# Sums of squares of four token tiles on ScalarE instead of TensorE, in a fused linear-attention and bilinear block

## The chip, the cores and the metric

The kernel runs on one core of a Trainium2 chip. The metric is device time in microseconds, of the whole kernel. A core has five engines with instruction queues of their own: TensorE (PE in the profile, with PEld for its weight loads), VectorE (DVE), ScalarE (ACT), GpSimd (POOL) and SyncE (SP), which here only issues transfers. Each works its queue off in order; they wait for each other through semaphores.

## The reference, cut to what matters

One batch of 2048 tokens of width 640 goes through a linear attention with 32 heads of 20 channels and a bilinear feed-forward of width 1536, both with a layer norm ahead and a residual around. All arrays are bf16.

```python
def _layernorm(x, axis=-1, eps=1e-5):
    m = jnp.mean(x, axis=axis, keepdims=True)
    v = jnp.var(x, axis=axis, keepdims=True)
    return (x - m) / jnp.sqrt(v + eps)
...
    qkv = (x @ wqkv) -> q, k, v per head
    pq = jnp.einsum("bhsd,hdf->bhsf", q, w_phi)
    pk = jnp.einsum("bhsd,hdf->bhsf", k, w_phi)
    phi_q = jnp.concatenate([_softmax(pq), _softmax(-pq)], axis=-1)
    phi_k = jnp.concatenate([_softmax(pk), _softmax(-pk)], axis=-1)
    kv = jnp.einsum("bhsf,bhsd->bhfd", phi_k, v)
    num = jnp.einsum("bhqf,bhfd->bhqd", phi_q, kv)
    o = num / den;  A(x) = o @ wo
    B(x) = ((x @ w_gate) * (x @ w_up)) @ w_down
...
    h = x + A(_layernorm(x));  h2 = h + B(_layernorm(h))
```

## The kernel before, in words

**Tiles.** Tokens are cut into 16 tiles of 128. A tile stands in the core's memory twice: `x_all` holds it as it is (tokens along the partitions), `xT` transposed (channels along the partitions), which is what a matmul needs. Both come from the same input by transfers that SP issues: `load_x(b)` brings four tiles of `x_all` at a time (units lx0 to lx3), `load_xT(t)` one transposed tile (units lT4 to lT15; tiles 0 to 3 are in unit "in").

**Statistics** (`stats`, units s0, s2, s4, s8, s12; the number is the first tile). The layer norm of the input needs a mean and a sum of squares per token. For most tiles TensorE multiplies a tile's transposed block by itself with a column of ones appended (128x129): the last column gives the sum, the diagonal the squares, and VectorE adds the diagonal up (L702). For the tiles in `ST_ACT` TensorE makes the sum alone (128x1), and ScalarE squares and sums the row from `x_all` (`act_sum`, L650). GpSimd then computes the scale from both (L707 to L719).

**Weights.** The key weights are folded with w_phi first (`wk_rounds`). Unit wk takes the mean of the key weights' rows and transposes them on TensorE (L746); two of the five blocks are copied out by VectorE (L784) and ScalarE (L787), the rest with the mean taken off (L803, L806). Meanwhile w_phi arrives as `Wrows`, by a transfer that stands in ScalarE's queue, and is spread into five block-diagonal pieces `Phi` by VectorE (three) and GpSimd (two), L636 in unit "in". Units x0 to x4 multiply the transposed key weights by `Phi`; x0 and x1 do so in two steps, the second with the mean repeated by GpSimd (L777). `evac` (L861, L864) writes the folded weights to `Wp`. The query weights follow the same way later (wm, wq, y0 to y4), value weights are centred by c0 to c4.

**Keys, values, queries.** Unit k (`keys`) multiplies a tile by the folded key weights, VectorE takes the row maximum (L925) and ScalarE two exponentials (L933); unit K normalises on VectorE and GpSimd. Unit v is the values, q and Q the queries, whose features go through two transposes on SP's queue (L1003). Units A sum keys times values over all tokens, then n, h, f and D are the attention's output, its projection, the feed-forward up and down.

**Order.** What runs when isn't found by the hardware: `ORDER` lists, for each engine, the units in sequence; where a unit has several instructions on an engine, its name stands several times and they are taken in the order in which the program makes them. In ScalarE's list "in" therefore means, in turn, the transfer of key weights, the transfer of `Wrows`, and one Exp on a column of ones (L612) that gets the table of functions loaded:

```python
load_wnat(1, (3, 5), "ACT", at=4.3)
load(Wrows[:, :, :], A_w_phi.rearrange(...), [R_Wrows], 0.03, eng="ACT", at=5.35)
...
g.op("ACT", lambda e: e.activation(out=junk[:, 0, 0:1], in_=ones[:, 0:1], func=ACT.Exp), ...)
```

`place` walks through the lists with assumed durations (`t`, `lat`, and for transfers `size`), to give buffers away; four double banks of matmul results (`p_ps`) are the scarcest. A transfer with `at` is taken there to arrive at that time, wherever its issue stands: `land = o.at or max(s + 2.3, fabric) + o.bytes`. `finish` then puts in the semaphores.

Of the kernel before, what the change touches and what calls it, by code (L numbers as in the profile page):

```python
# [11 lines left out]
P = 128  # L12
S = 2048
D = 640
NT = S // P
NC = D // P
# [41 lines left out]
ST_ACT = (12,)  # L58
# [39 lines left out]
    "DVE":  # L98
# [16 lines left out]
    "ACT":  # L115
# [318 lines left out]
def _build(ctx, nc, A_x, A_wqkv, A_w_phi, A_wo, B_w_gate, B_w_up, B_w_down, out):  # L434
    g = Prog(nc, ctx)
# [8 lines left out]
    x_all = sb([P, NT, D], BF16, "x_all")  # L444
# [1055 lines left out]
```

## Time and profile before

| what | value |
|---|---|
| median of 3 runs | 267.84 us (267.67 to 268.1) |
| the profiled execution | 267.55 us, span 265.8 us |
| TensorE busy | 260.4 us, 98% of the span |
| VectorE / ScalarE / GpSimd busy | 222.7 / 177.2 / 190.1 us |
| share of TensorE in the chain that ended last | 85% |
| granted clock of TensorE | 0.999 |
| transfers | 28.65 MB, mean 108 GB/s |

The span runs from the first to the last instruction of the profiled execution; its own time includes what lies around it. A busy share is an average over stages. The stages by time: weights up to about 12 us, keys, values and first queries up to 74 us, attention output and queries mixed with the feed-forward of the first 512 tokens up to about 150 us, then the feed-forward.

In timeline rows the columns are: start and length in us, engine, line, operation, result <- inputs, shape, count, and in brackets the idle time ahead of it with what ended it. A row can merge several instructions, and matmuls overlap, so that the step from start to start is what they cost. In the table by windows they are: window, its length, busy time and instruction count of PE, PEld, DVE, ACT and POOL, granted clock, share and rate of the transfers.

### The profile page before, as it was taken

The page shows a single profiled execution, that of the slowest core. Times are in us where ns is not written, and L with a number is a line of the kernel's source. Part 1 is how long each engine was busy: PE and PEld are TensorE (multiplying, and loading weights), DVE is VectorE, ACT ScalarE, POOL GpSimd, SP SyncE. Part 2 cuts the span into 40 slices and gives each one's busy share as a digit, 9 for nine tenths or more (in the row PEclk, how much of TensorE's full clock was granted, in tenths as well). Part 3 has the DMA queues.
Part 4 walks back from the last instruction along what each step waited for, and adds up shares of the span by engine and source line. Part 5 has one row for each costly group of instructions (what it writes and reads, how often), then busy time and mean ns, then how long its engine had stood idle before and what let it go on. Part 6 is the DMA issues. An engine that isn't in the chain of part 4 may idle for free.

```text
span 265.8 us, 6243 instructions
## 1 busy us (share of the span) xinstructions
PE 260.4 (98%) x2418; PEld 200.0 (75%) x2433; DVE 222.7 (84%) x417; ACT 177.2 (67%) x387; POOL 190.1 (72%) x243
## 2 busy tenths in 40 slices
PE   8999999999999999999999999999999999999995
PEld 8877777776877787777767887777777777777773
DVE  1999999999999876998999778988778788675683
ACT  2567999999857998769553695764857555645220
POOL 5446989999932889999974789359866575648652
PEclk9999999999999999999999999999999999999999
DMA  7997999903155789666856515300410401001012
GB/s 188 302 138 175 165 233 401 382 32 75 39 82 100 89 247 210 130 106 133 131 115 128 47 25 79 99 4 0 56 45 19 83 0 52 1 2 51 14 65 71
DMA packets 67390, 28.65 MB, mean 108 GB/s; under 512 B 57632, under 2 KB 66080, under 8 KB 67360
## 3 DMA queue, kind: packets, MB, share of 16 engines
q1 hardware_dynamic: 66432, 27.90, 48.7%
q10 hardware_dynamic: 928, 0.35, 0.5%
q8 instruction: 19, 0.31, 0.5%
q14 instruction: 11, 0.09, 0.1%
HBM read 11.82 MB, written 2.62 MB: 54 GB/s over the span
## 4 chain that ended last, share of the span: by engine, by line
PE 85%; DVE 5%; DMA 3%; ACT 3%; issue 1%; POOL 1%; SPq 0%; ACTq 0%
PE ps L657 60%; PE ps L1210 24%; DMA phiqT<-eq 3%; ACT eq L933 1%; DVE ob L1075 1%; PE ps L746 1%; DVE x_all L1093 1%; DVE ps L925 1%; DVE Sq L987 1%; ACT phiqT L1335 0%; POOL eq L999 0%; DVE rden L1073 0%; DVE phiqT L806 0%; ACT junk L650 0%; ACT eq L1220 0%
## 5 line engine op out<-in xcount | busy, mean ns | idle before, releaser
L657 PE MATMUL ps<-Wp,xT 128*128 128x320 bf16 (+1 forms) x606 | 89.1, 299 | 0.0
L657 PEld LDWEIGHTS ps<-Wp,xT 128*128 128x128 bf16 x606 | 58.0, 98 | 22.5 <-ACT phik L933 0.3
L1240 POOL TENSOR_TENSOR phik<-phik,gate 128x512 bf16<-128x512 bf16 x34 | 40.1, 1184 | 25.9 <-DVE phik L1237 25.5
L1220 ACT ACTIVATE eq<-ps 128x256 f32<-128x256 f32 x110 | 37.4, 386 | 23.0 <-PE ps L1210 18.6
L1210 PE MATMUL ps<-phik,Wgu 128*128 128x256 bf16 (+1 forms) x214 | 46.6, 299 | 0.2
L950 POOL TENSOR_TENSOR phik<-phik,Rk 128x1280 bf16<-128x1280 bf16 x16 | 37.4, 2357 | 5.8 <-DVE Rk L949 4.8
L657 PE MATMUL ps<-phik,Wgu 128*128 128x256 bf16 (+1 forms) x259 | 33.2, 280 | 0.1
L657 PEld LDWEIGHTS ps<-phik,Wgu 128*128 128x128 bf16 x260 | 25.0, 98 | 5.5
L1337 POOL TENSOR_TENSOR phiqT<-phiqT,x_all 128x320 f32<-128x320 f32 x26 | 21.7, 844 | 9.7 <-ACT phiqT L1335 9.6
L925 DVE TENSOR_REDUCE ps<-ps 128x1 f32<-128x640 f32 (+1 forms) x32 | 26.1, 818 | 2.8 <-PE ps L657 2.8
L1210 PEld LDWEIGHTS ps<-phik,Wgu 128*128 128x128 bf16 x228 | 21.9, 98 | 5.7 <-ACT eq L1220 0.2
L657 PE MATMUL ps<-vaug,phik 128*128 128x63 bf16 (+1 forms) x308 | 25.9, 238 | 0.0
L987 DVE TENSOR_REDUCE Sq<-eq 128x66 f32<-128x1320 bf16 x16 | 24.2, 1513 | 1.4 <-ACT eq L933 1.4
L1237 DVE TENSOR_TENSOR phik<-ps,eq 128x512 bf16<-128x512 f32 x28 | 19.1, 687 | 6.3 <-PE ps L1210 6.2
L1335 ACT ACTIVATE phiqT<-ps 128x320 f32<-128x320 f32 x26 | 11.4, 437 | 19.3 <-PE ps L657 19.2
L947 DVE TENSOR_REDUCE Ssum<-phik 128x64 f32<-128x1280 bf16 x16 | 23.3, 1460 | 0.0
L1235 DVE TENSOR_TENSOR gate<-ps,eq 128x512 bf16<-128x512 f32 x27 | 18.5, 685 | 5.2 <-PE ps L1210 2.9
L657 PEld LDWEIGHTS ps<-vaug,phik 128*128 128x128 bf16 x308 | 18.1, 97 | 5.3
L999 POOL TENSOR_TENSOR eq<-eq,rq 128x660 bf16<-128x660 bf16 x16 | 20.9, 1305 | 0.8
L933 ACT ACTIVATE eq<-ps,nb,rs 128x300 bf16<-128x300 f32 (+2 forms) x26 | 17.2, 689 | 6.1 <-DVE nb L928 4.5
L1342 DVE TENSOR_TENSOR outb<-ps,phiqT 128x320 bf16<-128x320 f32 x28 | 13.4, 487 | 6.9 <-PE ps L657 5.5
L1139 ACT ACTIVATE gate<-ps 128x256 bf16<-128x256 f32 (+1 forms) x26 | 10.4, 406 | 10.3 <-PE ps L657 9.6
(168 smaller groups left out, 526.2 us busy)
## 6 DMA issues: line engine op xcount, KB each, us to landing
x_all<-in_A_x_dram SPq DMA_DIRECT2D x4, 640.0 KB, 10.7
out_dram<-outb SPq DMA_DIRECT2D x14, 160.0 KB, 1.9
Wgu<-in_B_w_gate_dram SPq DMA_DIRECT2D x1, 1920.0 KB, 10.6
Wgu<-in_B_w_up_dram SPq DMA_DIRECT2D x1, 1920.0 KB, 16.3
vaug<-in_B_w_down_dram SPq DMA_DIRECT2D x1, 1920.0 KB, 8.5
Wp<-in_A_wqkv_dram SPq DMA_DIRECT2D x1, 800.0 KB, 5.0
phiqT<-in_A_wqkv_dram SPq DMA_DIRECT2D x1, 800.0 KB, 6.4
Wo<-in_A_wo_dram SPq DMA_DIRECT2D x1, 800.0 KB, 6.0
```

The lines of the kernel that those rows point to most:

```text
L657: ins = e.matmul(o_, lhsT=l_, rhs=r_, start=s_, stop=p_, skip_group_check=True)
L925: g.op("DVE", lambda e: e.tensor_reduce(out=mx(), in_=src(), axis=AX.XY if len(src().shape) == 3 else AX.X, op=ALU.max, apply_absolute_val ...
L933: g.op("ACT", lambda e, s=s, sc=sc, to=to, of=of: e.activation(out=to(s), in_=of(), func=ACT.Exp, bias=nb[:, i:i + 1], scale=sc[:, t:t + 1 ...
L947: g.op("DVE", lambda e: e.tensor_reduce(out=Ssum[:, vs.i, :], in_=x, axis=AX.X, op=ALU.add), rd=R_phik[t], wr=vs.R, use=[vs], t=1.39, lat=1.5)
L950: g.op("POOL", lambda e: e.tensor_tensor(out=x, in0=x, in1=Rk[:, vr.i, :].unsqueeze(2).to_broadcast([P, 2 * H, DH]), op=ALU.mult), rd=vr.R ...
L987: g.op("DVE", lambda e: e.tensor_reduce(out=Sq[:, vs.i, :].rearrange("p (w g) -> p w g", w=NQ), in_=feat(0, NQ).rearrange("p w (g f) -> p ...
L999: return e.tensor_tensor(out=x, in0=x, in1=rq[:, vr.i, :].rearrange("p (w h) -> p w h", h=HW).unsqueeze(3).to_broadcast([P, NQ, HW, DH]), ...
L1210: ins = e.matmul(o_, lhsT=l_[0](c), rhs=m_, start=fr, stop=False, skip_group_check=True)
L1220: g.op("ACT", lambda e: e.activation(out=half(s[i], 256 * h, 256 * (h + 1)), in_=PS[v.i][:, bk, 256:512], func=ACT.Copy), rd=[v.R[bk]], wr ...
L1237: g.op("DVE", lambda e: e.tensor_tensor(out=hhT[:, hb_, ft, :], in0=PS[v.i][:, 1, :], in1=half(s[1]), op=ALU.add), rd=[v.R[1]] + s[1].R, w ...
L1240: g.op(eng, lambda e: e.tensor_tensor(out=hhT[:, hb_, ft, :], in0=hhT[:, hb_, ft, :], in1=gate[:, vg.i, :], op=ALU.mult), rd=R_out + vg.R, ...
L1337: g.op("POOL", lambda e: e.tensor_tensor(out=slot(x), in0=slot(x), in1=x_all[:, t, c], op=ALU.add), rd=x.R + [R_h[t]], wr=x.R, use=[x], t= ...
```

## The change

`ST_ACT` gains tile group 8: tiles 8 to 11 get their sums of squares from ScalarE on `x_all` instead of from 128x129 products on TensorE and diagonal sums on VectorE. All five queues get a new order. Some of the assumed durations of `place` change (transfers are taken to land earlier, transposes to occupy less), which can change which buffer a unit gets, and nothing else that runs. Of the order the beginnings are shown, and SP's in full up to the queries; the later stages exchange neighbours.

```diff
-ST_ACT = (12,)
+ST_ACT = (8, 12)
...
     "PE":
-        "warm wk wk wk wk wk wk wk wk wk s0 wk x1 s0 x1 x3 wv wv x2 x0 x0 s2 x4 s2 k0 k0 k0 k0 k0 k3 k1 wm k2 v2 v3 s4 s4 s4 s4 "
-        "v5 k7 v7 k4 k6 v4 k5 y3 v0 y1 s8 s8 s8 s8 y4 k10 y2 y0 v1 s12 s12 k11 q0 s12 s12 k8 k9 v11 q1 v9 v6 k12 k13 v14 v10 v13 "
+        "warm wk wk wk wk wk wk wk wk wk wk s0 x1 s0 x1 x0 x3 x0 wv wv x2 x4 s2 s2 k0 k0 k0 k0 k0 k3 k1 wm v2 k2 v3 s4 s4 s4 s4 "
+        "k7 v5 v7 k4 v4 y3 k6 v0 y1 k5 s8 s8 s8 s8 y0 v1 y2 k10 y4 k11 s12 s12 s12 q0 s12 v11 k8 k9 v9 q1 k12 k13 v10 v14 v6 k14 "
...
     "DVE":
-        "wk in in wk in wk wk wk s0 s0 x1 x3 s0 c2 c1 c0 s2 s2 c4 s2 k0 k0 c3 k3 k3 k1 k1 K0 k2 wq2 wq4 K0 K1 k2 s4 s4 s4 s4 s4 "
+        "wk in in in wk wk wk wk s0 s0 s0 x3 x1 c1 c0 c2 s2 s2 k0 s2 k0 c3 c4 k3 k3 k1 wq2 k1 K0 k2 K0 k2 K1 s4 s4 s4 s4 s4 K3 k7 "
...
     "ACT":
-        "in in in wk wk wk x2 x0 x4 k0 k0 k3 wm k1 k1 v2 v3 k3 k2 wq1 k2 v5 wq3 k7 v7 k7 k4 k4 v4 k6 k6 k5 v0 k5 s12 y4 y2 s12 y0 "
+        "in wk in wk wk x0 x2 x4 in k0 k0 wm k3 k3 k1 v2 k1 wq1 v3 k2 s8 k2 s8 wq3 v5 k7 v7 k7 v4 k4 k4 s8 v0 s8 k6 k6 y0 k5 v1 "
...
     "POOL":
-        "in in in in in in in in in in in in pad in in wk s0 s0 s0 in in s0 s2 s0 s2 s2 s0 s2 s2 s2 K0 s4 s4 s4 s4 s4 s4 K3 K1 K2 "
+        "in in in in in in in in in in in in in in in wk s0 s0 s0 in s0 s0 in s2 s0 s0 s2 s2 s2 s2 s2 pad K0 s4 s4 s4 s4 s4 s4 K3 "
...
     "SP":
-        "in in in in in in in lwq t4 lT7 lT4 t2 lT5 lT6 t3 t1 t0 lx3 lT10 lT15 lT9 lT11 lT8 lT13 lT14 lT12 lx0 lwo lg lu lx2 lx1 "
-        "Q0 Q1 Q0 Q1 Q2 Q2 Q3 Q3 Q5 Q5 n2 n3 Q7 Q7 Q4 ld Q4 Q6 n7 n5 Q6 Q8 Q8 h3 n4 h2 Q10 Q10 n6 Q14 Q14 Q9 n8 Q9 h5 h7 Q11 Q11 "
+        "in in in in in in in t2 lwq lT6 t4 lT5 t1 lT4 lT7 lx2 t3 t0 lT14 lT10 lx0 lT11 lT9 lT8 lx3 lT13 lT12 lwo lT15 Q0 lg Q0 "
+        "lx1 Q1 lu Q1 Q2 Q2 Q3 Q3 Q5 n2 Q5 n3 Q7 Q7 ld Q4 Q4 Q6 n7 n5 Q6 h3 h2 Q8 Q8 n4 Q10 Q10 n6 Q14 Q14 n8 Q9 Q9 h7 h5 Q11 Q11 "
...
-        return g.op(eng, lambda e: e.dma_start(out_, in_), wr=wr, dma=("w", 8), t=0.5, lat=0.4 if at else 1.9, size=mb / 0.38, at=at)
+        return g.op(eng, lambda e: e.dma_start(out_, in_), wr=wr, dma=("w", 8), t=0.5, lat=0.4 if at else 0.6, size=mb / 0.38, at=at)
-    def transpose(out_, in_, rd, wr, use=(), t=1.27, size=1.07, lat=0.5, at=0.0):
+    def transpose(out_, in_, rd, wr, use=(), t=1.27, size=0.45, lat=0.3, at=0.0):
...
```

In the SP list "t" are transposed loads of query weights, lwq and lwo the query and output weights, lg, lu and ld the gate, up and down weights. The code of `stats` is the same; tiles 8 to 11 take its other branch.

More of the change, by code (lines that the diff above doesn't have):

```diff
@@ L587, in load_xT @@
     def load_xT(t, at=0.0):
-        transpose(lambda: xT[:, t, :, 0:P], lambda: A_x[0, P * t:P * (t + 1), :], [], [R_xT[t]], t=1.5, size=0.75, lat=1.25 if at else 2.75, at=at)
+        transpose(lambda: xT[:, t, :, 0:P], lambda: A_x[0, P * t:P * (t + 1), :], [], [R_xT[t]], t=1.5 if at else 1.4, size=0.75 if at else 0.62, lat=1.25 if at else 2.1, at=at)
     def load_x(b):
-        load(x_all[:, 4 * b:4 * b + 4, :], A_x[0, 4 * P * b:4 * P * (b + 1), :].rearrange("(t p) n -> p t n", p=P), [R_x[b]], 1.2)
+        load(x_all[:, 4 * b:4 * b + 4, :], A_x[0, 4 * P * b:4 * P * (b + 1), :].rearrange("(t p) n -> p t n", p=P), [R_x[b]], 0.9)
     def load_wv(c0, c1, at):
@@ L686, in f @@
                 return mms(e, lst)
-            g.op("PE", f, rd=[R_xT[t], R_one, R_xone], wr=[v.R[j // 2]], use=[v], t=0.125 if act else 0.282, lat=0.275 if act else 0.43)
+            g.op("PE", f, rd=[R_xT[t], R_one, R_xone], wr=[v.R[j // 2]], use=[v], t=0.19 if act else 0.282, lat=0.34 if act else 0.43)
             if act:
@@ L818, in wq_means @@
         v = Buf(p_ps, 2)
-        g.op("PE", lambda e: mms(e, mean_mms(PS[v.i][:, 0, :], range(NC), 0)), rd=R_Wnat + [R_one], wr=v.R, use=[v], t=0.64, lat=0.79)
+        g.op("PE", lambda e: mms(e, mean_mms(PS[v.i][:, 0, :], range(NC), 0)), rd=R_Wnat + [R_one], wr=v.R, use=[v], t=0.73, lat=0.88)
         g.op("ACT", lambda e: e.activation(out=nmeanq[:, :], in_=PS[v.i][:, 0, 0:NC], func=ACT.Copy, scale=-1.0 / SC),
@@ L1003, in queries @@
             SLOT_USERS.append(transpose(lambda w0=w0, w1=w1: phiqT[:, bb, w0:w1, P * tt:P * (tt + 1)], lambda w0=w0, w1=w1: eq[:, b.i, P * w0:P * w1],
-                      b.R + [R_pad], [R_phiqT[bb][k][tt]], [b], t=0.254 * (w1 - w0), size=0.214 * (w1 - w0)))
+                      b.R + [R_pad], [R_phiqT[bb][k][tt]], [b], t=1.3, size=0.5, lat=0.35))
     KVBUF = Buf(p_ps, 2)
@@ L1371, in wqT @@
         U("t%d" % a)
-        transpose(lambda: WT[:, 0, a, :], lambda: A_wqkv[:, P * a:P * (a + 1)], [], [R_WT[0][a]], t=1.5, size=0.75, lat=2.75)
+        transpose(lambda: WT[:, 0, a, :], lambda: A_wqkv[:, P * a:P * (a + 1)], [], [R_WT[0][a]], t=1.4, size=0.62, lat=2.1)
     U("warm")
@@ L1385, in _build @@
     U("lwo")
-    load(Wo[:, :, 0:D], A_wo.rearrange("(c p) n -> p c n", p=P), R_Wo, 1.5)
+    load(Wo[:, :, 0:D], A_wo.rearrange("(c p) n -> p c n", p=P), R_Wo, 0.95)
     for b in range(NB):
```

121 rows, old and new, of the table ORDER are left out of this document.

## The prediction

> **What bounds the kernel now.** I read the page first (busy shares, then the chain that ended last), then the table by windows for the stretch of keys and values, and then the timelines of single engines over the first 17 us, where the new order changes most.
>
> ```profile
> span 265.8 us, 6243 instructions
> PE 260.4 (98%) x2418; PEld 200.0 (75%) x2433; DVE 222.7 (84%) x417; ACT 177.2 (67%) x387; POOL 190.1 (72%) x243
> PE 85%; DVE 5%; DMA 3%; ACT 3%; issue 1%; POOL 1%; SPq 0%; ACTq 0%
> ...
> 20.00:40.00 20.00, 19.94 (x196) 15.30 (x194) 19.57 (x48) 18.16 (x27) 16.20 (x18) 1.00 0.87 193
> 40.00:60.00 20.00, 20.00 (x157) 14.28 (x155) 20.00 (x32) 18.99 (x30) 19.46 (x19) 1.00 0.72 268
> 60.00:74.00 14.00, 14.00 (x240) 11.25 (x238) 13.38 (x23) 12.01 (x20) 13.84 (x9) 1.00 0.27 54
> ```
>
> The reader should see two things. TensorE (PE) is the bound from end to end: 85% of the chain is its own work. And between 20 and 74 us VectorE (the third busy figure in a row, behind PE and PEld; ScalarE and GpSimd follow) is full too: 19.57 + 20.00 + 13.38 = 52.95 of 54 us. A microsecond in which TensorE stands still at the start therefore has no later slack to vanish in: it moves the end by a microsecond.
>
> **Part 1: twenty matmuls become narrow.** For tiles 8 to 11 the 128x129 products give way to 128x1 sums, as tiles 12 to 15 (s12) have them already.
>
> ```profile
> 34.13 1.30 PE L657 MATMUL ps<-xT 128*128 128x129 bf16 x20
> 35.26 0.48 PE L657 MATMUL ps<-Phi,phiqT 128*128 128x140 bf16 x6
> ...
> 39.20 0.39 PE L657 MATMUL ps<-ones,xT 128*128 128x1 bf16 x10
> 39.61 2.93 PE L657 MATMUL ps<-Wp,xT 128*128 128x320 bf16 x20
> 42.38 0.39 PE L657 MATMUL ps<-ones,xT 128*128 128x1 bf16 x10
> 42.63 1.11 PE L657 MATMUL ps<-Wp,xT 128*128 128x320 bf16 x7
> ```
>
> Start to start, s8 takes 35.26 - 34.13 = 1.13 us now. The same twenty in s12 take 0.41 + 0.25 = 0.66 us (at the faster of the two rates, 0.50). TensorE gains 0.47 to 0.63 us; I take **-0.5**. VectorE loses four diagonal sums. Each is 0.28 us long (the first row below), so four give back up to 1.1 us. That pays nothing while TensorE is full, but it keeps VectorE from becoming the bound.
>
> ```profile
> 13.28 0.28 DVE L702 CUSTOM_DVE_ANT_0 t<-ps,ident 128x128 f32<-128x128 f32 x1
> ...
> 36.23 0.74 ACT L650 ACTIVATE junk<-x_all 128x640 bf16<-128x640 bf16 x1
> 36.95 1.30 ACT L861 ACTIVATE Wp<-ps 128x640 bf16<-128x640 f32 x2
> ```
>
> **Part 2: ScalarE gets four squares.** One costs its queue 36.95 - 36.23 = 0.72 us, four 2.9 us, placed among keys 2, 7, 4 and 6. The table above leaves ScalarE idle for 20 - 18.16 = 1.84 us from 20 to 40, for 2.85 us from 20 to 60. So the cover just about holds: the cost lies between 0 and 2.9 - 1.84 = 1.1 us (if keys wait for their exponentials and TensorE for the banks behind them). I take **+0.1**, what is left over the idle of 20 to 60.
>
> The squares read x_all of tiles 8 to 11. That load stood behind lu and moves up in SP's queue, past twelve of the transposes that load xT and past lx3, lx0, lwo, lg and lu: seven transposes and lwq are left ahead of it behind the first seven entries.
>
> ```profile
> 22.46 0.58 SPq L549 DMA_DIRECT2D x_all<-in_A_x_dram  x1
> DMA to landing us min/median/max: 4.7/10.7/17.1
> ```
>
> The first x_all load went out at 22.46 us behind nine transposes and lwq; with two of about 1.3 us fewer this one goes out near 20. The four such loads took 4.7 to 17.1 us; the long ones went out behind the gate and up weights, which no longer stand ahead, so I take 4.7 and a landing near 25. The first square stands behind the first exponential of key 2, near 23.5 us plus the delay of part 3, so 27: zero. Without that delay ScalarE would wait up to 1.5 us.
>
> **Part 3: the load of Wrows now stands behind a waiting activation.** This decides. ScalarE's old order begins "in in in wk wk wk", the new one "in wk in wk wk x0 x2 x4 in". Of ScalarE, "in" is three things in this order: a load of key weights (L549), the load of Wrows (L549), the Exp that brings the table (L612). The first "wk" is the copy at L787. So the issue of Wrows moves behind L787, and ScalarE works in order.
>
> ```profile
> 0.78 0.46 ACTq L549 DMA_DIRECT2D phiqT<-in_A_wqkv_dram  x1
> 1.28 0.49 ACTq L549 DMA_DIRECT2D Wrows<-in_A_w_phi_dram  x1
> 1.80 1.28 ACT L612 ACT_TABLE_LOAD   x1 [1.80 <-issue]
> 6.44 0.70 ACT L787 ACTIVATE phiqT<-ps 128x640 bf16<-128x640 bf16 x1 [3.15 <-PE ps L746]
> 15.50 0.88 ACT L933 ACTIVATE phik<-ps,nb,rs 128x640 bf16<-128x640 f32 x1 [2.19 <-DVE nb L928]
> ...
> phiqT<-in_A_wqkv_dram ACTq DMA_DIRECT2D x1, 320.0 KB, 3.9
> Wrows<-in_A_w_phi_dram ACTq DMA_DIRECT2D x1, 25.0 KB, 4.6
> ...
> DMA to landing us min/median/max: 2.6/4.4/6.6
> ```
>
> L787 waits for TensorE's transposes until 6.44 us. So Wrows, now issued at 1.28 us and landed at 1.28 + 4.6 = 5.9 us, goes out between 6.44 us (behind the start of L787) and 7.14 us (behind its end). I take 6.5. How long it flies: 4.6 us was behind the 320 KB of its own queue, which landed at 0.78 + 3.9 = 4.7 us; the shortest of the early transfers takes 2.6 us (last line, the transposes). I take the middle, 3.6 us, and get a landing at **10.1 us**, bounds 6.44 + 2.6 = 9.0 and 7.14 + 4.6 = 11.7.
>
> The Trainium skill, "DMA: Bandwidth & Descriptors", section "Queues, rings and completion order", says that each DMA engine takes turns between the queue rows it has work for, packet by packet. By that rule the backlog of SP's queue would hardly hold the small load on ScalarE's row up, and the landing would lie at the lower bound of 9.0 us, with a delay of 2.4 us in place of the 3.5 us below.
>
> What waits for Wrows:
>
> ```profile
> 5.98 0.86 POOL L636 TENSOR_TENSOR Phi<-Wrows,G 128x140 bf16<-128x140 bf16 x2 [1.93 <-DMA Wrows<-in_A_w_phi_dram]
> 6.15 0.85 DVE L636 TENSOR_TENSOR Phi<-Wrows,G 128x140 bf16<-128x140 bf16 x2
> 7.36 0.17 DVE L775 TENSOR_SCALAR nmean<-ps 128x5 f32<-128x5 f32 x1 [0.36 <-PE ps L657]
> 7.44 0.32 DVE L636 TENSOR_TENSOR Phi<-Wrows,G 128x160 bf16<-128x160 bf16 x1
> 7.59 0.74 POOL L777 CAST outb<-nmean 128x640 bf16<-128x640 f32 x1 [0.75 <-DVE nmean L775]
> 7.86 0.47 PE L657 MATMUL ps<-Phi,phiqT 128*128 128x140 bf16 x6
> 8.17 0.45 PE L657 MATMUL ps<-xT 128*128 128x129 bf16 x5
> 8.45 0.48 PE L657 MATMUL ps<-Phi,outb 128*128 128x140 bf16 x6
> 9.14 0.47 PE L657 MATMUL ps<-Phi,phiqT 128*128 128x140 bf16 x6 [0.21 <-DVE sm L698]
> ```
>
> The first folded matmul of x1 (7.86 us) needs all five Phi pieces, three of them on VectorE. In the new order VectorE does the three in a row ahead of nmean: 0.85 + 0.32 us, plus some 0.1 for the two hand-overs, 1.25 us after the landing. x1 starts at 10.1 + 1.25 = 11.35 us, **3.5 us later** than 7.86 (bounds: 9.0 + 1.25 and 11.7 + 1.25, that is +2.4 and +5.1). TensorE has nothing else to do meanwhile: its queue holds s0 once ahead of x1, as before at 7.18 us, and s0, x1, x0, x3 and the value-weight sums behind it. nmean, now queued on VectorE behind the late Phi pieces, makes the cast at L777 late in turn: nmean and cast take 0.17 + 0.74 us after Phi, while TensorE has the first x1 and s0, 0.31 + 0.28 us, so a stall of about 0.3 us comes. It replaces the one ahead of 9.14 us (0.21 idle, and the pitch of 0.69 from 8.45), and I cost the difference at nothing. What follows, x0 to x4, s2 and key 0, moves as a block.
>
> The Exp with its table moves behind x4. The first activation is then L787, and the load of 1.28 us can stand ahead of it in ScalarE's 3.15 us of idle time. If it came behind L787's wait, Wrows would be later by 1.28 us; if it came ahead of key 0 it would lie in the 2.19 us before 15.50. Zero, inside the bounds.
>
> **Part 4: loads of gate and up weights.** lg, lx1 and lu now go out between the transposes of Q0 and Q1, and ld ahead of Q4's.
>
> ```profile
> 59.28 7.78 SPq L553 DMA_TRANSPOSE phiqT<-eq  x4
> 94.10 8.54 DMA phiqT<-eq
> 74.87 0.53 PE L657 MATMUL ps<-Phi,phiqT 128*128 128x42 bf16 x12 [0.29 <-DVE Phi L1040]
> L657 PE MATMUL ps<-phik,Wgu x150: 270/272/275, 85.6 to 120.9; 128*128 128x256 bf16 x150
> ```
>
> A transpose behind a big load lands late, 8.54 us (here behind ld). Q1's second half, issued by 59.28 + 7.78 = 67.1 us at the latest, would then land by 75.6; its user at 74.87 us moves to about 78. The gate weights, first used at 85.6, have 18 us. Zero; without the 3 us of delay up to 0.8 us.
>
> **Part 5: the rest of the order.** In all five queues many neighbours change places, the later stages included; the work is the same. TensorE is idle for 265.8 - 260.4 = 5.4 us of the whole span, the wait of 0.82 us at its start among it, so a better order can win little and a worse one has no row here to price it. I take zero, with 0.6 us either way in the range.
>
> **The sum.** The profiled execution took 267.55 us (span 265.8 and 1.75 around it), 0.29 under the median of 267.84. 267.55 + 3.5 - 0.5 + 0.1 = 270.65, so a median of **270.9 us**, 1.2% slower. With the bounds: 267.84 + 2.4 - 0.63 = 269.6, and 267.84 + 5.1 - 0.47 + 1.1 = 273.6.
>
> **Rivals.** *Not slower: the load is issued ahead of the wait.* If L787's wait holds only the arithmetic and the queue goes on to the next issue, Wrows still leaves near 1.3 us and the change is worth part 1: 267.84 - 0.5 = 267.3. For it: no separate semaphore instruction stands ahead of L787. Against: ScalarE's first three rows follow one another in order and none overlaps its predecessor's issue. It decides as soon as Wrows lands by about 6.5 us. Chance 0.10.
>
> *The clock falls.* TensorE would be idle from about 7.9 to 11.35 us. Early on it ran slowly:
>
> ```profile
> 0.82 4.21 PE L657 MATMUL ps<-const-bfloat16-1.0 128*128 128x128 bf16 x38 [0.82 <-PEq L1485]
> ```
>
> 38 matmuls of 128 columns in 4.21 us are 111 ns each; later the twenty of 129 columns in s8 take 1.13 us, 56 ns each. If the idle time sent TensorE back to that rate for as long as at the start (some 4 to 5 us), half of it would be lost: 2.0 to 2.5 us more, 273.1 us. Against: a stretch of that idle length is nowhere in this trace, so nothing shows it. Chance 0.10. The Trainium skill, "TensorE: Matmul & The Clock Gate", part 1, says that an idle window of about 3.4 us halves the clock and that the window runs freely; the idle time above is about that long, so it would be caught whole in few cases, and I keep the chance small.
>
> *ScalarE becomes the bound.* The squares find no gaps, and the whole 1.1 us of part 2 is paid: 267.84 + 3.5 - 0.5 + 1.1 = 271.9. For it: 18.99 of 20 us busy from 40 to 60. Against: 1.84 + 1.01 + 1.99 = 4.8 us idle from 20 to 74. Chance 0.10.
>
> **How the numbers follow.** Forecast 0.70, rivals 0.10 each. A measurement of this kernel tells changes of about 0.2% from none. Slower by more than that: forecast, clock and ScalarE, 0.90. The first rival ends at -0.2%, split into 0.06 faster and 0.04 same. Range 269.0 to 273.2: from the lower bound of the load's flight, less the 0.6 us of part 5, to the clock case; the upper bound of 273.6 needs every cost at its worst.
>
> **What would show it.** Wrows issued at 6.5 us or later on ScalarE's queue and landing near 10; Phi on GpSimd idle before that for over 5 us; the first matmul from Phi near 11.4 in place of 7.86; key 0's first matmul some 3.5 us after its old start; the 20 narrow matmuls of s8 in 0.5 to 0.7 us. Wrows landing before 7 would make the forecast wrong; a slow pitch of 128-column matmuls after the gap would show the clock; idle PE between 25 and 60 us ended by ScalarE would show the third.

## The result, and the profile after

The changed kernel takes **278.62 us** (median of 6 runs, 277.04 to 281.06), against 267.61 us for the kernel before on the same chip: ratio 1.0419, 95% interval 1.0373 to 1.0465. It is 11.0 us slower; 3.1 us had been forecast. The profiled execution of the changed kernel took 281.06 us with a span of 279.3, that of before 267.55 with 265.8. It is the slowest of the six, so what its trace loses (13.5 us of span) is 2.4 us more than the median does. Two markers are used below: key 0 is the start of the first 128x320 matmul of keys, and the end is that of the span.

The first part of the page of the changed kernel, and the chain that ended last by engine:

```profile
span 279.3 us, 6263 instructions
PE 263.7 (94%) x2433; PEld 200.3 (72%) x2433; DVE 226.3 (81%) x409; ACT 180.5 (65%) x395; POOL 190.9 (68%) x243
PE 59%; POOL 13%; DMA 11%; DVE 7%; ACT 5%; issue 2%; SPq 2%; ACTq 0%
```

TensorE is idle for 279.3 - 263.7 = 15.6 us, where it was 5.4 us before. Its share of the chain falls from 85 to 59%; transfers rise from 3 to 11%. The table by windows of the same kernel, and behind it three rows of the kernel before, say where (window, length, busy time of PE, PEld, DVE, ACT and POOL, granted clock, share and rate of the transfers):

```profile
0.00:20.00 20.00, 13.67 (x161) 12.38 (x162) 6.08 (x17) 4.54 (x7) 7.21 (x26) 0.83 0.97 207
20.00:40.00 20.00, 19.97 (x184) 14.78 (x184) 19.45 (x44) 17.17 (x28) 11.84 (x20) 1.00 1.02 219
40.00:60.00 20.00, 19.50 (x188) 14.05 (x186) 19.89 (x33) 20.00 (x35) 19.00 (x20) 1.00 0.12 14
...
74.00:100.00 26.00, 22.82 (x340) 18.34 (x337) 23.06 (x44) 18.13 (x37) 13.60 (x14) 1.00 0.60 143
100.00:150.00 50.00, 47.44 (x446) 36.19 (x444) 41.02 (x71) 37.44 (x82) 42.94 (x60) 1.00 0.80 142
```

```profile
0.00:20.00 20.00, 18.95 (x234) 16.14 (x235) 13.56 (x33) 9.47 (x14) 9.29 (x34) 1.00 1.03 209
74.00:100.00 26.00, 25.62 (x270) 20.41 (x267) 23.00 (x47) 21.48 (x51) 14.73 (x26) 1.00 0.70 137
100.00:150.00 50.00, 49.73 (x448) 37.44 (x448) 44.72 (x85) 31.93 (x68) 42.22 (x56) 1.00 0.75 127
```

Three places stand out. In the first 20 us 6.3 us are idle (1.05 before), and the granted clock is 0.83. From 74 to 100 us 3.2 us are idle (0.4 before), and from 100 to 150 us 2.6 us (0.3 before). The stretch that holds the squares, 20 to 60 us, loses 0.5 us. By markers the changed kernel is late by 7.25 us at key 0 (19.96 against 12.71), by 10.3 us at the first matmul of the output projection (88.87 against 78.56), and by 13.5 us at the end.

The start, from the timelines of the four engines, and last key 0 of the kernel before:

```profile
6.19 0.70 ACT L787 ACTIVATE phiqT<-ps 128x640 bf16<-128x640 bf16 x1 [3.62 <-PE ps L746]
6.20 0.38 ACTq L549 DMA_DIRECT2D Wrows<-in_A_w_phi_dram  x1
11.57 0.97 POOL L636 TENSOR_TENSOR Phi<-Wrows,G 128x140 bf16<-128x140 bf16 x2 [7.76 <-DMA Wrows<-in_A_w_phi_dram]
11.52 1.20 DVE L636 TENSOR_TENSOR Phi<-Wrows,G 128x140 bf16<-128x140 bf16 x3 [5.67 <-DMA Wrows<-in_A_w_phi_dram]
12.90 0.76 PE L657 MATMUL ps<-Phi,phiqT 128*128 128x140 bf16 x6 [5.25 <-DVE nmean L775]
13.45 0.75 PE L657 MATMUL ps<-xT 128*128 128x129 bf16 x5
...
16.39 2.46 PE L657 MATMUL ps<-Wp,ones 128*128 128x320 bf16 x10
18.69 0.79 PE L657 MATMUL ps<-Phi,phiqT 128*128 128x140 bf16 x12
...
19.96 0.72 PE L657 MATMUL ps<-Wp,xT 128*128 128x320 bf16 x4
```

```profile
12.71 4.25 PE L657 MATMUL ps<-Wp,xT 128*128 128x320 bf16 x30
```

The issue of `Wrows` leaves ScalarE just after the start of L787, as forecast. The data lands at 11.50, and the first matmul of x1 starts 1.40 us later, at 12.90 in place of 7.86. The six matmuls then take 0.76 us, where the same group took 0.47 before: the clock has fallen. Its record shows 0.50 from 11.47 to 18.30 us. From x1 to key 0 it takes 7.06 us; before, the same matmuls in another order took 12.71 - 7.86 = 4.85. So the delay of 7.25 us at key 0 is 5.04 us of late data and 2.2 us of slow clock.

The queries' transposes, in the view of DMA issues from 60 to 82 us (KB each, median us to landing), and TensorE's timeline behind them:

```profile
Wgu<-in_B_w_gate_dram SPq DMA_DIRECT2D x1, 1920.0 KB, 8.5
Wgu<-in_B_w_up_dram SPq DMA_DIRECT2D x1, 1920.0 KB, 9.2
x_all<-in_A_x_dram SPq DMA_DIRECT2D x1, 640.0 KB, 10.6
phiqT<-eq SPq DMA_TRANSPOSE x5, 5.5
```

```profile
83.56 0.52 PE L657 MATMUL ps<-Phi,phiqT 128*128 128x42 bf16 x12 [1.71 <-DMA phiqT<-eq]
83.92 1.56 PE L657 MATMUL ps<-Wp,xT 128*128 128x300 bf16 x10
86.94 0.44 PE L564 MATMUL ps<-ident,ob 128*128 128x128 bf16 x5 [1.46 <-DVE nb L928]
```

Q1's second transpose went out at 72.58 us and landed at 83.43. TensorE stood 1.71 us for it and 1.46 us for VectorE behind it: the 3 us between the first two markers.

### The profile page after: what moved, and what is told of

Same layout as the page of the kernel before. It is cut to its first block, busy times and chain, and to the rows that moved or that the text cites. A ratio compares the mean times of both kernels' runs of the same rounds, so it can differ in the third digit from the quotient of the medians.

```text
span 279.3 us, 6263 instructions
## 1 busy us (share of the span) xinstructions
PE 263.7 (94%) x2433; PEld 200.3 (72%) x2433; DVE 226.3 (81%) x409; ACT 180.5 (65%) x395; POOL 190.9 (68%) x243
## 4 chain that ended last, share of the span: by engine, by line
PE 59%; POOL 13%; DMA 11%; DVE 7%; ACT 5%; issue 2%; SPq 2%; ACTq 0%
PE ps L657 35%; PE ps L1210 24%; DMA phiqT<-eq 8%; POOL phik L950 7%; ACT eq L933 3%; DMA Wrows<-in_A_w_phi_dram 2%; POOL eq L999 2%; DVE Sq L987 2%; DMA phiqT<-in_A_wqkv_dram 2%; SPq L553 1%; POOL rs L1113 1%; ACT junk L650 1%; DVE ps L925 1%; POOL rs L714 1%; POOL phik L1145 1%
## 5 line engine op out<-in xcount | busy, mean ns | idle before, releaser
L1210 PE MATMUL ps<-phik,Wgu 128*128 128x256 bf16 (+1 forms) x228 | 50.6, 304 | 0.0
L657 PE MATMUL ps<-phik,Wgu 128*128 128x256 bf16 (+1 forms) x260 | 34.0, 281 | 0.2
L1235 DVE TENSOR_TENSOR gate<-ps,eq 128x512 bf16<-128x512 f32 x26 | 17.7, 686 | 6.3 <-PE ps L1210 3.3
L657 PE MATMUL ps<-Phi,phiqT 128*128 128x63 bf16 (+3 forms) x236 | 13.3, 205 | 7.1 <-DVE nmean L775 5.2
L1139 ACT ACTIVATE gate<-ps 128x256 bf16<-128x256 f32 (+1 forms) x26 | 10.2, 402 | 12.5 <-PE ps L657 11.4
```

The lines of the kernel that those rows point to most:

```text
L657: ins = e.matmul(o_, lhsT=l_, rhs=r_, start=s_, stop=p_, skip_group_check=True)
L1210: ins = e.matmul(o_, lhsT=l_[0](c), rhs=m_, start=fr, stop=False, skip_group_check=True)
```

## The experiments

The theory after the result had three terms: the late `Wrows`, the clock that falls in the idle time it makes (7.25 us in the trace, the two together), and the loads of gate, up and down weights ahead of the transposes. Rivals to it were that the squares or the new order cost the time, that the late start also makes the later waits, and that the start is made good later. That the later order itself holds 2 to 3 us became the theory only when the first experiments had left that much over. Each ratio is against the kernel before on the same chip. Differences of medians below can be of runs on two chips; the kernel before took 267.51 to 267.73 us on them, so 0.2 us of such a difference mean nothing.

**The start alone.** The old order, with nothing but the copy at L787 moved ahead of the issue of `Wrows` and the Exp:

```diff
-        "in in in wk wk wk x2 x0 x4 k0 ...   # before, ACT
+        "in wk in in wk wk x2 x0 x4 k0 ...
```

> The kernel before with one exchange in ScalarE's order: the copy at L787 ahead of the load of Wrows and the Exp, all else as it was. Theory (the late load makes the start late by itself, 5.0 us at x1 and, with the slow clock, 7.25 us at key 0): Wrows goes out near 6.4 us and lands near 11.5 us, key 0 near 19 to 20 us, time 273 to 275 us, since TensorE is full behind it. Rival (only the new order makes it expensive): Wrows just as late, but under 270 us.

Measured: 274.34 us, ratio 1.0248 (1.0218 to 1.0278). From PE's timeline:

```profile
12.62 0.76 PE L657 MATMUL ps<-Phi,phiqT 128*128 128x140 bf16 x6 [4.79 <-DVE Phi L636]
...
18.75 0.99 PE L657 MATMUL ps<-Wp,xT 128*128 128x320 bf16 x6
```

Key 0 is 6.04 us late, and the end is 6.03 us late in the same execution (271.83 against 265.80). What is lost at the start arrives at the end one for one: nothing later has the slack to take it back. One name moved in one list costs 6.6 us by the medians; the Exp, which moved with it, took 0.20 us at 6.85 us, while ScalarE had nothing else to do.

**The start undone.** The changed kernel with the old beginning of ScalarE's list:

```diff
-        "in wk in wk wk x0 x2 x4 in k0 k0 wm ...   # after, ACT
+        "in in in wk wk wk x0 x2 x4 k0 k0 wm ...
```

> The changed kernel with the start of ScalarE's order alone put back: the load of Wrows and the Exp ahead of the copy at L787. Theory (three separate costs: Wrows late, the clock that falls in the idle time it makes, and the loads of gate, up and down weights ahead of feature transposes): Wrows lands near 5.9 us, x1 starts near 7.7 us, key 0 near 12.7 us, all 128-column matmuls after that at 56 ns; the time falls by the 7.25 us of the start in the profiled execution, somewhat less in the median, to 271 to 273 us, and the waits in the middle (0.5 us or more, between 80 and 155 us) stay. Rival (the late start also makes the waits of the middle, since everything there meets out of step): 267 to 268 us.

Measured: 272.98 us, ratio 1.0204 (1.018 to 1.0228): 5.6 us of the 11.0 are back. Key 0 is at 12.36, 0.35 us ahead of before. It is still 2.74 us late at the output projection and 5.7 us late at the end, so what is lost later does not hang on the start.

**Why `Wrows` flies 5.3 us.** In the changed kernel, SP's load of the value weights is made to wait for L787, so that SP's queue holds less when `Wrows` goes out:

```diff
-    load_wv(0, 5, 9.15)
+    late_wv = load_wv(0, 5, 9.15)
...
+    late_wv.deps[<L787's op>] = False
```

> The changed kernel with one more dependency: the transfer of the value weights on SP's queue (800 KB), and with it all that SP issues behind, waits until the copy at L787 is done. The load of Wrows then goes out with only two early transposed tiles ahead of it. Theory (the small load queues behind all that was issued earlier on SP, though it stands on ScalarE's queue): its flight falls from 5.3 us to 3.3 us or less, x1 starts near 11 us. Rival (a load of 640 rows of 40 bytes takes 5 us by itself): flight 4.8 us or more. The time is not what this run is for, since the value weights come later.

Measured: 278.05 us, ratio 1.0387 (1.0361 to 1.0413). Its DMA issues up to 14 us, and PE's timeline:

```profile
Wrows<-in_A_w_phi_dram ACTq DMA_DIRECT2D x1, 25.0 KB, 3.2
```

```profile
10.86 0.76 PE L657 MATMUL ps<-Phi,phiqT 128*128 128x140 bf16 x6 [3.02 <-DVE nmean L775]
...
14.35 2.42 PE L657 MATMUL ps<-Wp,ones 128*128 128x320 bf16 x10
...
17.88 1.40 PE L657 MATMUL ps<-Wp,xT 128*128 128x320 bf16 x9
```

Issued at 6.27 us in place of 6.20, `Wrows` now takes 3.2 us in place of 5.3, and x1 starts 2.04 us earlier. So SP's transfers made the flight long. That it waited behind those issued before it, and did not share the engines with them, is in the trace of the changed kernel: from 6.20 to 9.7 us not one packet of ScalarE's queue moved, while SP's kept the 16 engines full, and from 9.7 to 10.9 us all 25 KB did. The load landed at 11.50, after the third transpose of `xT`, which SP had issued 1.2 us ahead of it (landed at 10.75), and before the fourth (11.69). The whole time hardly fell (two runs, 277.44 and 278.67). In the slower one, which was profiled, the clock fell all the same: 7.02 us from x1 to key 0. The other had a mean clock of 0.999 and was only 1.2 us faster; the later value weights may hold it up, which isn't shown.

**The clock.** TensorE is kept busy with repeated transposes of a weight block whose results are overwritten, ahead of x1; the first run does the last block 15 times over, the second 21 times (shown):

```diff
-                for a in range(NC):
+                for a in [a for _ in range(21 if c == NC - 1 else 1) for a in range(NC)]:
```

> The changed kernel with the last block of transposes in the key weights' round (L746, five matmuls) done fifteen times over, the same values into the same place: 70 more matmuls of 128 columns, 3.9 us, in TensorE's idle time before Wrows lands. Theory (the idle time lets the clock fall): x1 starts as late as in the changed kernel, near 12.9 us, but its matmuls run at 60 ns in place of 107 ns, key 0 comes near 17.7 us, granted clock 1.0 in all runs, time 276 to 277 us and less spread. Rival (the slow matmuls there have another cause, such as late inputs): key 0 near 20 us, time 278 to 279 us.

> The changed kernel with the last block of transposes done twenty-one times over, 100 more matmuls, 5.6 us, so that TensorE is idle for less than 2 us before Wrows lands. Theory (idle time of about 3 us or more makes the clock fall): x1 starts near 13 us, the sums of the value weights run at 136 ns per matmul, key 0 comes 4.9 us after x1 and not 7, granted clock 1.0 in all runs, time 276 to 277.5 us. Rival (the slow stretch has another cause): 7 us from x1 to key 0, 278 to 280 us.

With 15 repeats: 279.22 us, ratio 1.0393 (1.0345 to 1.0442), where 276 to 277 had been expected. It settled little: `Wrows` landed at 12.81, TensorE still stood 2.66 us, and the clock still fell. With 21 repeats: 277.96 us, ratio 1.041 (1.0369 to 1.0452), just above the 276 to 277.5 expected. PE's timeline and the window of the first 20 us of this run:

```profile
6.86 6.02 PE L746 MATMUL ps<-ident,phiqT 128*128 128x128 bf16 x105
12.71 0.45 PE L657 MATMUL ps<-xT 128*128 128x129 bf16 x5
14.65 0.47 PE L657 MATMUL ps<-Phi,phiqT 128*128 128x140 bf16 x6 [1.49 <-DVE nmean L775]
...
16.78 1.52 PE L657 MATMUL ps<-Wp,ones 128*128 128x320 bf16 x10
...
19.41 4.25 PE L657 MATMUL ps<-Wp,xT 128*128 128x320 bf16 x30
```

```profile
0.00:20.00 20.00, 17.44 (x265) 16.25 (x266) 6.53 (x18) 5.09 (x8) 7.23 (x26) 1.00 1.02 194
```

Now the clock stays at 1.00, and x1 to key 0 takes 4.76 us in place of 7.06: the fall of the clock costs **2.3 us**. A second sign is in the runs of the filler kernels: with 15 repeats, the run with a mean clock of 1.000 took 276.23 us and the three with 0.992 to 0.994 took 278.93 to 280.34; with 21 repeats, three runs with 0.999 to 1.000 took 277.54 to 278.19 and one with 0.994 took 280.71. The median gained nothing over the changed kernel, because the data came still later: `Wrows` landed at 13.24, and the third transpose of `xT` ahead of it at 12.49 in place of 10.75. Why SP's transposes come later when TensorE runs filler was not found.

The price depends on how long the clock stays down, and that comes in steps. The record of the clock shows 0.50 for 6.83 us in the changed kernel (11.47 to 18.30) and in the one without the backlog (9.35 to 16.18), but for 3.4 us in the start alone (12.64 to 16.06) and with 15 repeats (14.89 to 18.30), so for one or two times 3.41 us. One step cost 1.28 us (the start alone, 18.75 - 12.62 against 4.85), two cost 2.3. In these profiled runs a mean clock of 0.988 goes with two steps, and 0.992 to 0.994 with one. All six runs of the changed kernel have 0.987 to 0.994, and the two at 0.994 are its fastest (277.04 and 277.12); the clock does not explain the whole spread, since a run at 0.987 took 277.90 and one at 0.988 took 281.06.

**The gate and up loads ahead of the transposes.** In the changed kernel, lg and lu go back in front of Q0:

```diff
-        ... lwo lT15 Q0 lg Q0 lx1 Q1 lu Q1 Q2 ...   # after, SP
+        ... lwo lT15 lg lu Q0 Q0 lx1 Q1 Q1 Q2 ...
```

> The changed kernel with lg and lu alone moved, both ahead of Q0's first transpose; ScalarE's order stays. Theory: the transposes of Q1 fly 2.6 to 2.8 us in place of 10.8, the wait of 1.71 us for a transpose near 83.5 us and the 1.6 us behind it go, time 275 to 276.5 us. Rival (the waits of the middle come from the squares on ScalarE and the new order): 278 to 279 us, waits of the same length ended by ScalarE or VectorE.

Measured: 277.46 us, ratio 1.0362 (1.0332 to 1.0393), which by itself is not clear of the changed kernel's interval, and short of the 275 to 276.5 us expected. With the start undone as well:

> Both edits: ScalarE's start put back, lg and lu ahead of Q0. Theory: start and Q transposes as in the kernel before; only ld ahead of Q4's transposes is left, so 267.5 to 269.5 us. Rival (new order or squares cost the middle): above 271 us.

Measured: 270.96 us, ratio 1.0122 (1.0101 to 1.0142), 2.0 us under the start undone alone, and the intervals are apart. The 267.5 to 269.5 us expected were missed: these two are not all of the loss. DMA issues from 60 to 82 us and PE's timeline of the run with the loads alone moved:

```profile
phiqT<-eq SPq DMA_TRANSPOSE x5, 2.6
```

```profile
81.78 0.53 PE L657 MATMUL ps<-Phi,phiqT 128*128 128x42 bf16 x12 [0.29 <-DVE Phi L1040]
82.14 1.56 PE L657 MATMUL ps<-Wp,xT 128*128 128x300 bf16 x10
83.54 0.44 PE L564 MATMUL ps<-ident,ob 128*128 128x128 bf16 x5
```

The five transposes take 2.6 us at the median in place of 5.5, and both waits of the changed kernel (1.71 and 1.46 us) are gone; the 0.29 us that is left stood there before the change. The delay no longer grows between 74 us and the output projection (6.91 us at both).

**The down weights.** With both of these undone, ld goes back behind the first transpose of Q4:

```diff
-        ... Q5 n3 Q7 Q7 ld Q4 Q4 Q6 ...
+        ... Q5 n3 Q7 Q7 Q4 ld Q4 Q6 ...
```

> The changed kernel with ScalarE's start put back, lg and lu ahead of Q0, and ld behind Q4's first transpose, as in the kernel before. Theory (the down weights ahead of Q4's transposes cost the 1.07 us of idle TensorE at 106.4 us, and part of what follows): 268.5 to 270 us, 1 to 2 us less than without this last edit. Rival (the later order itself costs what is left over the kernel before): 270.5 to 271.5 us, as without it.

Measured: 270.28 us, ratio 1.0106 (1.0086 to 1.0126), not to be told from the run before it, and above the 268.5 to 270 us expected. ld is not the rest.

**The squares alone.** In the old order, tiles 8 to 11 go to ScalarE, with lx2 moved ahead of the later transposes of xT, VectorE's four diagonal sums gone from its list, and the four squares put by hand between keys 7, 4, 6 and 5:

```diff
-ST_ACT = (12,)
+ST_ACT = (8, 12)
...
-        ... k7 v7 k7 k4 k4 v4 k6 k6 k5 v0 ...   # before, ACT
+        ... k7 v7 k7 s8 k4 k4 s8 v4 k6 s8 k6 s8 k5 v0 ...
-        ... t3 t1 t0 lx3 lT10 lT15 lT9 lT11 lT8 ... lg lu lx2 lx1   # before, SP
+        ... t3 t1 t0 lx2 lT10 lT9 lT11 lT8 lx3 lT15 ... lg lu lx1
```

> The kernel before, old order, with the squares of tiles 8 to 11 on ScalarE and the few moves that this needs: the x_all load of these tiles goes out where that of tiles 12 to 15 went, that one after four transposes more, the four squares stand among keys 7, 4 and 6 on ScalarE. Theory (part 1 of the prediction): TensorE loses 0.5 us, ScalarE has just room, 267.1 us. Rival (ScalarE becomes the bound): up to 1.1 us on top, 268.2 us or more.

Measured: 270.6 us, ratio 1.0116 (1.0096 to 1.0135), against 267.1 expected. The window of 30 to 44 us of this run, then PE's waits from 30 to 42 us (in total, times, longest), and last the same window of the kernel before:

```profile
30.00:44.00 14.00, 11.48 (x123) 8.35 (x122) 11.43 (x17) 14.00 (x27) 11.69 (x12) 1.00 1.10 280
```

```profile
PE ps L657 <- DVE sm L698: 0.9, 1, 0.9
PE ps L657 <- ACT vaug L956: 0.8, 1, 0.8
PE ps L657 <- ACT phik L933: 0.5, 1, 0.5
```

```profile
30.00:44.00 14.00, 13.94 (x147) 10.56 (x145) 13.97 (x32) 13.05 (x22) 12.88 (x13) 1.00 0.92 262
```

Here ScalarE (the fourth busy figure) is full: 14.00 of 14 us, before 13.05. Two of TensorE's waits end on its exponentials and values; the third is on the copy of sums by VectorE. The twenty narrow matmuls of s8 take 0.50 us from start to start, as forecast, and are outweighed. To see how much of this is ScalarE's time, the squares were cut short:

```diff
-                act_sum(x_all[:, t, :], ACT.Square, ...)
+                w_ = 64 if i0 == 8 else D
+                ... activation(out=junk[:, vj.i, 0:w_], in_=x_all[:, t, 0:w_], func=ACT.Square, ...)
```

> The kernel before with the squares of tiles 8 to 11 alone (270.6 us), each square over 64 of the 640 channels only, so the sums of squares of these tiles leave nine tenths out; loads, order and the narrow products on TensorE as there. Theory (ScalarE's 2.9 us of squares between keys 7 and 5 are paid by TensorE, which waits for the banks that ScalarE empties): a square shrinks by 576 columns, some 0.5 us each, 2 us in all, and the time falls to 268 to 269 us. Rival (the moved loads of x_all or the order on VectorE cost it): 270 to 271 us.

Measured: 269.45 us, ratio 1.007 (1.0054 to 1.0086). Some 1.15 us come back, and ScalarE is no longer full (13.30 of the 14 us). That is ScalarE's part, with a reserve: three of the six runs with whole squares and two of the four with short ones had a mean clock of 0.994, and among those at full clock the medians are 269.74 and 268.99, 0.75 us apart. Why the clock fell in the others isn't shown, since both profiled runs kept it. In all, 1.9 us against the kernel before stay, among them a wait of 0.97 us for VectorE at 36.90 us. They come from the new place of the squares and loads in the lists; which of the moves, no run tells.

**The squares in the new order.** The kernel of the down-weights run, with tiles 8 to 11 back on TensorE:

```diff
-ST_ACT = (8, 12)
+ST_ACT = (12,)
...
-        ... k2 s8 k2 s8 wq3 ... s8 v0 s8 k6 ...   # ACT; DVE gets its four diagonal sums back
+        ... k2 k2 wq3 ... v0 k6 ...
```

> The kernel with ScalarE's start put back, lg and lu ahead of Q0 and ld behind Q4's first transpose (270.3 us), with tiles 8 to 11 done on TensorE and VectorE again, in the same new order. Theory (the squares are hidden in the new order, the loss lies in the later order): 270 to 271 us, 0.5 us more at most for the wide products. Rival (the squares make the loss): 267.5 to 268.5 us.

Measured: 271.33 us, ratio 1.0153 (1.0127 to 1.018), about 1 us slower than with the squares on ScalarE (270.28, 1.0086 to 1.0126; the intervals barely part). So in the new order the squares cost nothing, and what this order still loses is not theirs.

**The later order undone.** The same kernel with the lists of before from n0, Q5 and Q7 on; the squares and the new order up to there stay:

```diff
-        ... A12 A14 n0 n1 n1 n0 q7 n0 q4 n1 ... f0.10.0 f0.10.0 f0.4.0 f0.4.0 ...   # after, PE; likewise DVE, ACT, POOL, SP
+        ... A12 A14 n0 n1 n0 n1 q7 n0 q4 n1 ... f0.4.0 f0.4.0 f0.10.0 f0.10.0 ...
```

> The changed kernel with ScalarE's start put back, lg and lu ahead of Q0, and from the attention output on (n0, or Q5 and Q7 on SP's and GpSimd's queues) the order of the kernel before. Squares on ScalarE and the new order of the first 74 us stay. Theory (what is left of the loss, 2.5 to 3 us, comes from the new later order, between 100 and 145 us): 267 to 268.2 us. Rival (the squares cost it, through ScalarE): 270 us or more.

Measured: **267.94 us**, median of 11 runs, ratio 1.0012 (1.0001 to 1.0023): 0.12% over the kernel before, by an interval that just leaves out no change. So the later order holds the rest, 270.28 - 267.94 = 2.3 us (2.5 by the ratios). The changed assumptions of `place` are in this kernel too, so they are not what costs the time. The windows from 100 to 145 us of the kernel with the new later order:

```profile
100.00:120.00 20.00, 18.69 (x172) 14.13 (x170) 15.24 (x30) 13.44 (x31) 17.14 (x24) 1.00 0.80 136
120.00:145.00 25.00, 24.78 (x210) 17.02 (x208) 22.20 (x40) 16.83 (x33) 21.50 (x27) 1.00 0.68 122
```

and of the one with the old later order:

```profile
100.00:120.00 20.00, 20.00 (x192) 15.40 (x189) 17.20 (x33) 15.30 (x34) 19.09 (x30) 1.00 0.85 157
120.00:145.00 25.00, 25.00 (x220) 18.18 (x218) 23.14 (x43) 15.72 (x32) 20.28 (x24) 1.00 0.69 125
```

TensorE is idle for 1.5 of these 45 us in the one, with 382 matmuls, and for none in the other, with 412. The largest single loss of the new order is seen in its timelines of ScalarE and TensorE:

```profile
105.06 0.45 ACT L1139 ACTIVATE gate<-ps 128x256 bf16<-128x256 f32 x1
107.17 0.60 ACT L933 ACTIVATE eq<-ps,nb,rs 128x300 bf16<-128x300 f32 x1 [1.67 <-DMA phiqT<-eq]
107.67 0.37 ACT L1139 ACTIVATE gate<-ps 128x256 bf16<-128x256 f32 x1
107.94 0.66 ACT L1143 ACTIVATE phik<-ps 128x256 bf16<-128x256 f32 x2
105.64 1.54 PE L657 MATMUL ps<-Wo,vaug 128*128 128x320 bf16 x10
108.38 1.54 PE L657 MATMUL ps<-Wp,xT 128*128 128x300 bf16 x10 [1.19 <-ACT phik L1143]
```

ScalarE's next entry is an exponential whose buffer is held until a transpose (`phiqT<-eq`) has landed. It stands 1.67 us, and behind it in its queue are the exits of two feed-forward banks (L1139, L1143). TensorE needs those banks and stands 1.19 us. The same wait for L1143 is 2.0 us long in the changed kernel. Where the other 1.1 us or so of the later order are lost, and which exchange of neighbours does it, was not tried.

**The account.** By medians, and from the kernel before up: later order 2.3 (270.28 less 267.94), gate and up loads 2.0 (272.98 less 270.96), start 5.6 (278.62 less 272.98). These make 9.9 us of the 11.0. The rest is the 0.4 us of the last kernel over before and the 0.7 us between the two kernels that differ in ld, whose intervals overlap; neither is explained. The 2.3 us of the clock are inside the 5.6 of the start.

## Why the prediction was right or wrong

The direction and the place that "decides" were right; the size was short by 7.7 us (278.62 against 270.9, above the range's 273.2). By the steps below these are the flight of `Wrows` (1.5), the clock (2.2), part 4 (2.0) and part 5 (2.3), 8.0 in all, the first two from the slowest execution and the others from medians. The late data alone, 5.04 us at x1, lay inside the bounds of 2.4 to 5.1 given for it; the time left the range by the other three, which the sum left out or held at nothing. Point by point, by the prediction's steps.

*What bounds.* Right: TensorE has no later slack. With the start alone moved, 6.04 us at key 0 are 6.03 us at the end.

*Part 1, narrow matmuls, -0.5.* Right: 0.50 us in the squares-alone kernel, and the new order without the squares is slower by about 1 us, not faster.

*Part 2, squares, +0.1.* Right for the order that the change brings: lx2 went out at 19.92 us and landed at 24.43 (forecast near 20 and 25), and the stretch from 20 to 60 us lost 0.5 us of TensorE. Its bound of 1.1 us was no bound of the edit in any order, though: put by hand into the old order it cost 3.0 us, of which some 0.75 to 1.15 are ScalarE's time, near that bound; the rest goes with the new places in the lists, which the bound left out. (lx2 moves past eight transposes of xT, not twelve; the seven left ahead of it are right, and nothing hangs on it.)

*Part 3, `Wrows`, +3.5.* The mechanism was right in each link: issue at 6.20 (forecast 6.5), x1 1.40 us behind the landing (forecast 1.25), TensorE with nothing else to do. **The term that failed is the flight**, taken as 3.6 us, the middle of 2.6 and 4.6 us. It was 5.3 us. The 2.6 us was misread as that of an early transfer: it is a transpose of query features, issued at 59.28 us, and those issued in the first 14 us took 3.8 us or more. And at 6.2 us SP had just issued the 800 KB of value weights and a transposed load. Taking those away gave 3.2 us, near the forecast, so the price of the load itself was right, and its queue was left out. The Trainium skill, "DMA: Bandwidth & Descriptors", section "Queues, rings and completion order", has each DMA engine take turns between the queue rows it has work for, from which the prediction worked out a landing at 9.0 us. The traces do not bear that landing out: no packet of this load moved before 9.7 us, it landed at 11.50, behind a transfer that another queue had issued before it, and at 9.45 only once SP's transfers were held back. The measurement decides; whether the load's row had work to offer the engines before 9.7 us, no run shows.

*The rival "the clock falls", 0.10.* It came true, on top of the forecast and not in its place: granted clock 0.83 in the first 20 us, 2.3 us by the run that kept TensorE busy (forecast 2.0 to 2.5). Its price was right for a fall of two steps; its chance was too low. The flight that was too short made the idle time too short (forecast 3.45 us, measured 5.25), but 3.02 us lost the clock too, so the forecast's own 3.45 us was not safe. The Trainium skill, "TensorE: Matmul & The Clock Gate", part 1, names an idle window of about 3.4 us that runs freely. An idle time of 5.25 us lost the clock, as the rule has it; but so did 3.02 us, and 2.66 us in the profiled run with 15 repeats, both shorter than that window, while 1.49 us did not, nor did 2.02 us ahead of L1143's banks in the changed kernel. Nor is it the length alone: of the kernels with 3.02 and 2.66 us one run each had a mean clock of 0.999 to 1.000.

*Part 4, the loads among the transposes, 0.* **Wrong**, by 2.0 us of the median. The prediction took one transpose behind one big load (8.5 us) and found its user by then 3 us late itself. Q1's second half stood behind both gate and up weights and took 10.85 us, and as its issue shifted with the delay at the start, the user's delay bought nothing: the two waits stay when the start is undone (1.2 and 1.5 us).

*Part 5, the rest of the order, 0 within 0.6.* **Wrong**, by 2.3 us. "A worse one has no row here to price it" was true, but the 0.6 us was then no bound. The order of before had only 0.27 us of TensorE idle between 100 and 150 us (49.73 of 50 busy), so there was all to lose: an order that exchanges ScalarE's entries there could lose whole waits for transposes, each of 1 to 2 us, as one did.

*The other rivals.* "Not slower: the load is issued ahead of the wait" fell: the issue follows L787's start by 0.01 us, so ScalarE works in order, transfers included. "ScalarE becomes the bound" fell for this change (the squares cost nothing in its order) and is what happens in part when they are put into the old one.

## What to carry to other kernels

A transfer whose issue stands in a compute engine's queue inherits every wait of that engine: before its entry is moved past an instruction, look up when that instruction starts, what other queues have issued by then, and who stands idle meanwhile. Price a small load by what is ahead of it on all queues, not by its own size, and small transposes the same way when megabytes of weights go out between them. Where a stall of TensorE reaches some 2.5 us, add the slow clock that can follow it, here 1.3 to 2.3 us.

## What the runs showed of the hardware that was not expected

A load of 25 KB on ScalarE's queue took 3.2 us when SP's queue had little ahead of it, and 5.0, 5.3, 6.6 and 7.1 us in kernels where SP's value weights and a transpose stood before it; in the changed kernel none of its packets moved for the first 3.5 us. Transposes between two loads of 1.9 MB took 5.5 us at the median and up to 10.85, against 2.6 without. TensorE lost its clock at idle times of 2.66 and 3.02 us, though not in every run, kept it at 1.49 and 2.02 us, and was then at 0.50 for one or two times 3.41 us; behind 5.25 us of idle this was 6.83 us, some 5.4 of them with matmuls. In the kernel with 3.02 us it fell at 9.35 us, only 1.5 us into the idle time, and with 15 repeats at 14.89, when TensorE was at work again: so the moment of the fall is set by more than the length of the idle time. A longer run of filler matmuls on TensorE went with later landings of SP's transposes (the third at 10.75, 11.85 and 12.49 us with 1, 15 and 21 repeats); nothing here says why.
